# Layer 1 in five token blocks, and remainders stacked along the contraction

## The chip, the cores and the metric

The kernel runs on one core of a Trainium2 chip. The metric is the device time of one execution in microseconds (us), as the median of several. TensorE (PE) multiplies matrices, with its weight loads counted apart (PEld); VectorE (DVE), ScalarE (ACT) and GpSimd (POOL) do the elementwise work; SyncE (SP) issues the DMAs.

## The reference

```python
# attention with 8 heads, 4 batches, 576 tokens, head dimension 64
proj = q_or_k @ w_phi;  proj -= max|proj|;  phi = [exp(proj), exp(-proj)]
x = (phi(q) @ (phi(k).T @ v)) / (phi(q) @ sum(phi(k)) + 1e-6)     # heads side by side: 512 wide
# layer 1
u  = x + real(fft(fft(x, axis=tokens), axis=features))
un = (u - mean(u)) / sqrt(var(u) + 1e-6)
x  = u + maximum(un @ w_ch1, 0) @ w_ch2                           # 512 -> 2048 -> 512
# layer 2
u  = x + (maximum(x.T @ w_tok1, 0) @ w_tok2).T                    # over tokens, 576 -> 256 -> 576
out = u + maximum(u @ w_ch1, 0) @ w_ch2                           # 512 -> 1536 -> 512
```

All is float32. The kernel gets this accuracy from a rounded type (`fp32r`): a number is split into a high and a low half (`h`, `l`), and a product is three matmuls, high by high, high by low and low by high.

## The kernel before

Tokens or features lie along the partitions, a batch is 576 tokens, and a half batch of 288 tokens is the unit of a normalization. The stages run one into the other.

The attention fills the first 190 us. Behind each batch follows its Fourier part. `f_fold` adds and subtracts mirrored tokens into `f`, `f_st1` and `f_stx` multiply by a cosine or sine table over the features (plain float32, four matmuls of 129 columns per call of `f_st1`, L624, each of them two records in the trace), and `f_st2` by one over the tokens. The even part has 289 rows and the odd part 287, each in two tiles of 128 rows and a remainder of 33 or 31. `f_stx` makes the remainders (`yxh`, `yxl`). `f_st2` (L672) adds nine matmuls of 290 columns into one bank of PSUM, three for each of the two full tiles and three for the remainder, which fill only about a quarter of the array's rows. It is called five times per batch, 20 times in all, and L677 and L678 add its result to `u`.

`ln` normalizes half a batch. A ones matrix (L920) sums over the 512 features, for the mean and then for the variance. Ahead of it VectorE adds the four feature tiles up (L911, L913; for the later halves ScalarE and GpSimd split the sum for two faster matmuls). VectorE subtracts the mean (L947), ScalarE squares, and after the second matmul come the root (L965 to L974, VectorE and ScalarE) and the product (L978). `ln_out` splits the result into `xh` and `xl` (ScalarE L995, GpSimd L998).

Layer 1 takes eight blocks of 288 tokens in the batch order 1, 2, 3, 0. `ch1` makes one of 16 tiles of 128 hidden features with 12 matmuls (L1015), ScalarE writes `gh` (L1022), VectorE `gl` (L1023), and `ch2` multiplies them by the second weights into four banks, 12 matmuls (L1037 to L1039). A group is four hidden tiles, after which VectorE adds the four banks to `u` (L1042, four additions). So layer 1 has 3072 matmuls of 288 columns and 128 additions. The first three blocks take the groups 0 to 3 in turn, the next three 3 to 0, the last two 0 to 3.

The weights come through "words": SP loads `raw`, ScalarE, VectorE (L1596: one TENSOR_SCALAR and two SCALAR_TENSOR_TENSOR on 128x512) and GpSimd make halves of it. Two groups of four stay in SBUF; the words of groups 2 and 3 are made while the first blocks run, `w_keep` stores them to DRAM (32 DMAs), and `w_fetch` reads a half group of 1 MB back (`w<-wd`, 24 times).

Layer 2 follows: `c_tr` transposes the tokens to the partitions, `c_tok1` multiplies by `w_tok1` with 512 columns (L1340 to L1342), five tiles of tokens for each of four batches, where the fifth has 64 tokens; then `c_tok2`, and from 698 us the channel product of layer 2, which the change leaves as it is.

Nothing of the order is found at run time. A table `ORDER` gives each step of the attention, the Fourier part and the beginning of layer 1 a start number (its scale only sorts), later steps get theirs from `at` and `later`, and all are emitted in the order of these numbers, which is the order in each engine's queue. An engine works its queue strictly in that order, so a wait holds everything behind it.

## Time and profile before

| | us |
|---|---|
| median of 3 runs (990.99, lowest 989.68, highest 991.08) | 990.99 |
| the profiled execution | 991.51 |
| its span, first to last instruction | 989.8 |
| TensorE busy, 98% of the span | 969.8 |
| VectorE busy, 70% | 689.4 |
| ScalarE busy, 43% | 427.5 |
| GpSimd busy, 41% | 407.9 |

Times are of one profiled execution. The busy time of a matmul counts its whole passage, and successive matmuls overlap, so TensorE may be busy with others' tails; what one matmul costs is read from the distance of the starts. "Idle before" is the time in which an engine stood still ahead of an instruction, and the arrow names what released it. The granted TensorE clock is full (1.00 of 2.4 GHz) in every stretch read here.

### The profile page before, as it was taken

Reading aid. Unit: us, or ns where it says so; the run is one execution under the profiler, and the core shown is the slowest. Engines: PE = TensorE matmul, PEld = TensorE weight load, DVE = VectorE, ACT = ScalarE, POOL = GpSimd, SP = SyncE. Lnnn points to the kernel's source line nnn. Section 1 sums busy time; section 2 is a strip of 40 time slices with the busy share of each in tenths; the row PEclk is TensorE's granted clock in tenths of the full one; section 3 lists DMA queues with packets and bytes.
Section 4 is the critical chain, followed back from the end, with each engine's and each line's share of the span. In section 5 each row is a group of like instructions: output and inputs, shape, how many; then the busy total and the mean of one; then the engine's idle time right before and its main releaser. Section 6 shows DMA issues by size and latency. Waiting matters only on the chain.

```text
span 989.8 us, 21218 instructions
## 1 busy us (share of the span) xinstructions
PE 969.8 (98%) x8322; PEld 905.5 (91%) x8322; DVE 689.4 (70%) x1275; ACT 427.5 (43%) x952; POOL 407.9 (41%) x429
## 2 busy tenths in 40 slices
PE   8999999999999999999999999999999999999998
PEld 8677867789988999999999999988899999999997
DVE  6898898998698845545666843467566768766665
ACT  5676566552244322322333322243444456544442
POOL 0150312131144523333445643332366568865651
PEclk9999999999999999999999999999999999999999
DMA  8566666627155723577334597780045455744452
GB/s 315 185 192 227 193 213 198 226 82 256 57 200 172 243 97 109 175 282 271 129 111 151 192 387 282 235 281 1 4 154 181 154 166 165 243 151 150 150 160 96
DMA packets 97727, 179.04 MB, mean 181 GB/s; under 512 B 9316, under 2 KB 53796, under 8 KB 94044
## 3 DMA queue, kind: packets, MB, share of 16 engines
q1 hardware_dynamic: 97468, 177.62, 53.3%
q8 instruction: 66, 1.08, 0.5%
q14 instruction: 33, 0.27, 0.1%
q10 hardware_dynamic: 160, 0.07, 0.0%
HBM read 126.65 MB, written 48.57 MB: 177 GB/s over the span
## 4 chain that ended last, share of the span: by engine, by line
PE 86%; DVE 9%; ACT 2%; issue 2%; POOL 1%; DMA 0%; SPq 0%; DVEq 0%; ACTq 0%; POOLq 0%
PE pw L1015 18%; PE pw L1107 12%; PE pz L1116 11%; PE pw L434 4%; PE pa L550 3%; PE pk L458 3%; PE pk L1038 3%; PE pk L1039 3%; PE pk L1037 3%; PE pa L1037 3%; PE pa L1039 3%; PE pa L1038 3%; DVE t L1596 3%; PE pw L672 3%; PE pa L530 2%; PE pw L497 2%
## 5 line engine op out<-in xcount | busy, mean ns | idle before, releaser
L1015 PE MATMUL pw<-xh,w 128*128 128x288 f32 x896 | 196.7, 295 | 0.0
L1171 DVE TENSOR_TENSOR u<-u,pz 128x576 f32<-128x576 f32 x157 | 118.1, 753 | 61.2 <-PE pz L1116 59.1
L1107 PE MATMUL pw<-x,ring 128*128 128x288 f32 x1008 | 155.4, 297 | 3.2 <-DVE f L1129 3.2
L1023 DVE SCALAR_TENSOR_TENSOR gl<-pw,gh 128x288 fp32r<-128x288 f32 x128 | 58.1, 455 | 133.3 <-ACT gh L1022 132.9
L1022 ACT ACTIVATE gh<-pw 128x288 fp32r<-128x288 f32 x128 | 52.2, 411 | 227.5 <-PE pw L1015 203.9
L1015 PEld LDWEIGHTS pw<-xh,w 128*128 128x128 f32 x896 | 149.9, 188 | 0.2
L1116 PE MATMUL pz<-g,ring 128*128 128x288 f32 x966 | 149.3, 298 | 0.6 <-DVE u L1171 0.5
L1107 PEld LDWEIGHTS pw<-x,ring 128*128 128x128 f32 x1008 | 139.5, 188 | 6.5 <-DVE f L1129 4.6
L1116 PEld LDWEIGHTS pz<-g,ring 128*128 128x128 f32 x966 | 134.3, 188 | 4.3 <-DVE u L1171 3.3
L1015 PE MATMUL pw<-xl,w 128*128 128x288 f32 x448 | 132.2, 295 | 0.0
L1596 DVE SCALAR_TENSOR_TENSOR t<-raw,t 128x512 uint32<-128x512 uint32 (+3 forms) x130 | 100.9, 781 | 2.2
L1596 POOL TENSOR_TENSOR g<-t,g 128x288 fp32r<-128x288 f32 (+1 forms) x69 | 71.0, 1030 | 42.1 <-ACT g L1142 42.1
L1015 PEld LDWEIGHTS pw<-xl,w 128*128 128x128 f32 x448 | 84.1, 188 | 0.1
L1596 ACT ACTIVATE f<-f 128x288 f32<-128x288 f32 x72 | 32.0, 444 | 116.3 <-DVE f L1129 115.9
L1596 POOL TENSOR_TENSOR g<-f,g 128x288 fp32r<-128x288 f32 x69 | 57.0, 841 | 59.5 <-ACT g L1142 59.4
L1038 PE MATMUL pk<-gl,w 128*128 128x288 f32 x256 | 76.3, 298 | 3.3 <-DVE gl L1023 3.1
L1037 PE MATMUL pk<-gh,w 128*128 128x288 f32 x256 | 76.4, 299 | 1.7 <-DVE u L1042 0.9
L1039 PE MATMUL pk<-gh,w 128*128 128x288 f32 x256 | 75.7, 296 | 0.0
L1037 PE MATMUL pa<-gh,w 128*128 128x288 f32 x256 | 75.6, 295 | 0.0
L1039 PE MATMUL pa<-gh,w 128*128 128x288 f32 x256 | 75.4, 295 | 0.0
L1038 PE MATMUL pa<-gl,w 128*128 128x288 f32 x256 | 75.1, 293 | 0.0
L768 POOL TENSOR_TENSOR wst<-t,wst 128x512 fp32r<-128x512 f32 x16 | 21.4, 1344 | 117.7 <-ACT wst L765 117.7
(212 smaller groups left out, 2095.5 us busy)
## 6 DMA issues: line engine op xcount, KB each, us to landing
w<-wd SPq DMA_DIRECT2D x24, 1024.0 KB, 5.7
ring<-wd SPq DMA_DIRECT2D x24, 1024.0 KB, 5.5
raw<-in_w SPq DMA_DIRECT2D x32, 512.0 KB, 5.5
ring<-wd SPq DMA_DIRECT2D x24, 512.0 KB
wd<-wst SPq DMA_DIRECT2D x22, 448.0 KB, 4.4
wd<-raw SPq DMA_DIRECT2D x22, 448.0 KB, 3.0
wd<-wst SPq DMA_DIRECT2D x18, 512.0 KB, 3.9
wd<-w SPq DMA_DIRECT2D x32, 256.0 KB, 2.8
```

Source lines behind the costliest of these rows:

```text
L434: nc.tensor.matmul(ps[j][:, (t - t0) * 128:(t - t0 + 1) * 128], x[h], T["w"][h], start=True, stop=True)
L458: nc.tensor.matmul(out[g:g + 64], e[:, g:g + 64], v, start=first, stop=last)
L1015: nc.tensor.matmul(out, w[:, k, fs], x[:, k, :], start=(n == 0), stop=(n == 11))
L1022: nc.scalar.activation(out=gh, in_=out, func=AF.Relu)
L1023: nc.vector.scalar_tensor_tensor(out=gl, in0=out, scalar=0.0, in1=gh, op0=ALU.max, op1=ALU.subtract)
L1037: nc.tensor.matmul(out, wh[:, f % 4, ds], gh, start=(f == f0), stop=False)
L1038: nc.tensor.matmul(out, wh[:, f % 4, ds], gl, start=False, stop=False)
L1039: nc.tensor.matmul(out, wl[:, f % 4, ds], gh, start=False, stop=last)
L1107: nc.tensor.matmul(out, w[:, kk, hw], x[XI[i]][:, hx, kk], start=(start and k == 0), stop=(stop and k == 5), skip_group_check=(i != 2))
L1116: nc.tensor.matmul(o[s], w[:, s, hw], g[hx], start=(start and k == 0), stop=(stop and k == 2), skip_group_check=(i != 2))
L1171: nc.vector.tensor_tensor(out=u, in0=u, in1=o, op=ALU.add)
L1596: fn(*a, **k)
```

## The change

The blocks of layer 1 become five, of 512, 512, 512, 480 and 288 tokens, across the borders of batches (`BLOCKS`). Blocks 0 and 1 are done first (`ROUND1`): block 0 with group 0, in two parts of 288 and 224 columns; block 1 with groups 0 and 1; block 0 with 1 and 2; block 1 with 2 and 3; block 0 with 3. Blocks 2, 3 and 4 follow with groups 3 and 2, and again with 1 and 0. Except for the first and last of round 1, eight hidden tiles are accumulated before `u` is added to. An addition is cut where a block crosses two batches. `w_keep` goes; groups 2 and 3 stay, and 0 and 1 are fetched again, group 1 half way through block 4.

Block 1 needs the fourth half, (2, 1), so its normalization joins the three early ones, with its product on GpSimd. Batch 0 is read back as `u0`, normalized from that copy between its spill and its use, stored (`un`) and loaded again before its blocks.

In the Fourier part `f_three` copies the remainder's columns of `f` three times side by side (two ScalarE copies per batch). `f_stx` thus leaves three copies of the 33 or 31 rows, of which `hi` and `third` make (high, high, low), and the table's remainder holds (high, low, high). One matmul over 99 or 93 rows then does what three did: seven in place of nine in `f_st2`. In the token product the fifth tile of 64 tokens is stacked in the same way in two copies, four matmuls in place of six per batch, with one more ScalarE copy (`c_two`).

```diff
-ps_open/a/k -99.600, opn/cv -99.500, a_open -99.000, a_warm/12#2 -98.100, a_load/0/k/0 -98.090, a_load/0/k/1 -98.080,
+ps_open/a/k -99.600, a_open -99.500, thirds -99.000, opn/cv -98.100, a_load/0/k/0 -98.090, a_warm/12#2 -98.080,
...
+    def third(out, src, k, w, n):
+        nc.vector.scalar_tensor_tensor(out=out, in0=src, scalar=T["z"][0:n, k, w:w + 1], in1=out, op0=ALU.mult, op1=ALU.add)
...
+    def f_three(b):
+        need(("fold", b, 0), ("fold", b, 1))
+        for w in range(2):
+            s0, n = (COS_T, SIN_T)[w][2]
+            a, e = (3, 5) if w else (0, 3)
+            nc.scalar.copy(out=T["fx"][:, a:e, 0:3 * n].rearrange("p a (r t) -> p a r t", r=3),
+                           in_=T["f", b][:, a:e, s0:s0 + n].unsqueeze(2).to_broadcast([128, e - a, 3, n]))
+        mark("three", b)
...
+                    nc.tensor.matmul(ps[0:3 * n, par * 129:(par + 1) * 129], T["fx"][:, fi, 0:3 * n],
...
+        def hi():
+            for w, n, ps, y in out:
+                nc.scalar.activation(out=y, in_=ps, func=AF.Copy, scale=T["z"][0:n, 2, w:w + 1])
+            mark("hi", "y", b)
+
+        def lo():
+            need(("hi", "y", b))
+            for w, n, ps, y in out:
+                third(y, ps, 0, w, n)
+            mark("y", b)
+        later(V('da', 1.0), hi)
+        later(V('db', 1.5), lo)
...
-            yh, yl = (y[:, w if st_ == 2 else st_] for y in T[("yx", b) if st_ == 2 else ("y", b, w)])
-            for y, c in ((yh, ch), (yh, cl), (yl, ch)):
-                nc.tensor.matmul(ps[0:m, 0:290], y[:, k0:k0 + m], c[:, st_, :],
-                                 start=(n == 0), stop=(n == 8))
+            if st_ == 2:
+                prods = [(T["yx"][:, w], ch)]
+            else:
+                yh, yl = (y[:, st_] for y in T["y", b, w])
+                prods = [(yh, ch), (yh, cl), (yl, ch)]
+            for y, c in prods:
+                nc.tensor.matmul(ps[0:m, 0:290], y[:, k0:k0 + m], c[:, st_, :], start=(n == 0), stop=(n == 6))
...
-    def w_keep(g, which, k):
-
-        if (0, g, which) not in WD:
-            WD[0, g, which] = dr.tile([2, 128, 4, 512], F32, name=f"wd0{g}{which}")
-        need(("w", 0, g, which, k))
-        mark("wd", ("w", 0, g, which, k))
-        for c in range(2):
-            nc.sync.dma_start(out=WD[0, g, which][c][:, k], in_=W[0, g][which][c][:, k].bitcast(F32))
...
-    FIRST = [(1, 0), (1, 1), (2, 0)]
+    FIRST = [(1, 0), (1, 1), (2, 0), (2, 1)]
+    BLOCKS = [[(1, 0, 512)], [(1, 512, 64), (2, 0, 448)], [(2, 448, 128), (3, 0, 384)], [(3, 384, 192), (0, 0, 288)],
+              [(0, 288, 288)]]
+    ROUND1 = [(0, (0,)), (1, (0, 1)), (0, (1, 2)), (1, (2, 3)), (0, (3,))]
...
+        u = (U[b] if b else T["u0"])[:, :, hf * HB:(hf + 1) * HB]
...
-            (nc.vector if (b, hf) in FIRST else nc.gpsimd).tensor_tensor(out=c, in0=c, in1=r.unsqueeze(1).to_broadcast([128, 4, HB]), op=ALU.mult)
+            (nc.vector if (b, hf) in FIRST[:3] else nc.gpsimd).tensor_tensor(out=c, in0=c, in1=r.unsqueeze(1).to_broadcast([128, 4, HB]), op=ALU.mult)
+            if b == 0:
+                spill["un", hf] = dr.tile([128, 4, HB], F32, name=f"un{hf}")
+                return later(V('us', 2.0), nc.sync.dma_start, out=spill["un", hf], in_=c)
...
+    def parts(blk, g):
+        return [(0, 288), (288, 224)] if blk == 0 and g == 0 else [(0, NB[blk])]
...
+    def u0_load():
+        P["ln"] = pool("ln", 1, "right")
+        T["u0"] = P["ln"].tile([128, 4, S], F32, name="u0")
+        nc.sync.dma_start(out=T["u0"], in_=spill[0])
+
+    def un_load(hf):
+        T["un", 0, hf] = P["tmp"].tile([128, 4, HB], F32, tag="c", name="un")
+        nc.sync.dma_start(out=T["un", 0, hf], in_=spill["un", hf])
...
+                o = -c0
+                for b, t, n in BLOCKS[blk]:
+                    lo, hi = max(o, 0), min(o + n, w_)
+                    if lo < hi:
+                        u = U[b][:, d, t + lo - o:t + hi - o]
+                        nc.vector.tensor_tensor(out=u, in0=u, in1=out[:, lo:hi], op=ALU.add)
+                    o += n
...
+    def c_two(b):
+        t = T["ud", b] = P["cb"].tile([128, 4, 2, 64], F32, tag="ud", name="ud")
+        nc.scalar.copy(out=t, in_=U[b][:, :, 512:576].unsqueeze(2).to_broadcast([128, 4, 2, 64]))
...
-            nc.tensor.matmul(out, h1[0:n, kt, cs], h[0:n], start=(kt == 0), stop=False)
-            nc.tensor.matmul(out, h1[0:n, kt, cs], l[0:n], start=False, stop=False)
-            nc.tensor.matmul(out, l1[0:n, kt, cs], h[0:n], start=False, stop=(kt == 4))
+            nc.tensor.matmul(out, h1[:, kt, cs], h, start=(kt == 0), stop=False)
+            if kt < 4:
+                nc.tensor.matmul(out, h1[:, kt, cs], l, start=False, stop=False)
+            nc.tensor.matmul(out, l1[:, kt, cs], h, start=False, stop=(kt == 4))
...
-    NS = 3
-    for n in range(NS):
-        at(zl + V(f'ln{n}', (36, 54, 74)[n]), ln, *blocks[n], (0, 1, 1)[n])
-        at(zl + V(f'lo{n}', (50, 68, 90)[n]), ln_out, *blocks[n], "dve" if n == 0 else "pool")
...
+    for n, (h, gs) in enumerate(ROUND1):
+        ts = t0
+        t0 = chan(0, t0, four(*gs), h, V(f'fb{n}', (8.0, 5.4, 5.18, 5.18, 5.18)[n]))
...
-    tx = {}
-    for g in (3, 2, 1, 0):
-        for h in ((3, 4, 5) if g else (5, 3, 4)):
-            tx.setdefault(h, t0)
-            chan(0, t0, list(range(4 * g, 4 * g + 4)), blocks[h], fin=(g == 0))
-            t0 += 4 * FT
-        if g > 1:
-            refill(g - 2, t0)
...
+    for h, gs in ((2, (3, 2)), (3, (2, 3)), (4, (3, 2)), (2, (1, 0)), (3, (0, 1)), (4, (1, 0))):
+        ts = t0
+        t0 = chan(0, t0, four(*gs), h)
+        if h == 4 and gs[0] > 1:
+            refill(1, (ts + t0) / 2)
+            refill(0, t0)
+        if h == 2:
+            tb3 = t0
...
+    at(zend + V('p00', 50.0), ln, 0, 0, 2)
+    at(zend + V('p01', 84.0), ln, 0, 1, 2)
+    tcv2 = zend + V('p02', 118.0)
+    at(tcv2, rel, "ln")
+    at(tcv2 + 0.1, opr, "cv2")
+    at(tb2 - 78, ln, 3, 0, 2)
+    at(tb2 - 42, ln_out, 3, 0, 0)
+    at(tb2 - 39, ln, 3, 1, 2)
+    at(tb2 - 6, ln_out, 3, 1, 0)
+    at(tb2 - 5.5, ln_out, 3, 1, 1)
+    at(tb2 + 2, un_load, 0)
+    at(tb2 + 14, ln_out, 0, 0, 0)
+    at(tb2 + 17, un_load, 1)
+    at(tb2 + 30, ln_out, 0, 1, 0)
```

The first place is TensorE at one `f_st2` in the attention. `sch` and `scl` are the halves of the cosine table, `yh`, `yl`, `yxh`, `yxl` those of the first product. Before:

```order
L624 MATMUL pw<-dsin,f 128x129 x4
L672 MATMUL pw<-sch,yh 128x290
L672 MATMUL pw<-scl,yh 128x290
L672 MATMUL pw<-sch,yl 128x290
L672 MATMUL pw<-sch,yh 128x290
L672 MATMUL pw<-scl,yh 128x290
L672 MATMUL pw<-sch,yl 128x290
L672 MATMUL pw<-sch,yxh 128x290
L672 MATMUL pw<-scl,yxh 128x290
L672 MATMUL pw<-sch,yxl 128x290
```
and now:
```order
L569 MATMUL pa<-qe,kz_104 64x288 x4
L716 MATMUL pw<-sch,yh 128x290
L716 MATMUL pw<-scl,yh 128x290
L716 MATMUL pw<-sch,yl 128x290
L716 MATMUL pw<-sch,yh 128x290
L716 MATMUL pw<-scl,yh 128x290
L716 MATMUL pw<-sch,yl 128x290
L716 MATMUL pw<-sch,yx 128x290
```
Nine matmuls of 290 columns are seven, the last with the stacked `yx`.

The second place is VectorE just behind the last Fourier sums of batch 2 (L677, now L720). Before:

```order
L677 TENSOR_TENSOR u<-u,pw 128x289
L678 TENSOR_TENSOR u<-u,pw 128x287
L695 COPY u<-x_3650 1x576
L1042 TENSOR_TENSOR u<-u,pk 128x288 x2
L1042 TENSOR_TENSOR u<-u,pa 128x288 x2
L657 TENSOR_TENSOR yl<-pw,yh 128x258
L1023 SCALAR_TENSOR_TENSOR gl<-pw,gh 128x288 x2
L677 TENSOR_TENSOR u<-u,pw 128x289
L678 TENSOR_TENSOR u<-u,pw 128x287
L677 TENSOR_TENSOR u<-u,pw 128x289
L678 TENSOR_TENSOR u<-u,pw 128x287
L677 TENSOR_TENSOR u<-u,pw 128x289
```
and now:
```order
L720 TENSOR_TENSOR u<-u,pw 128x289
L721 TENSOR_TENSOR u<-u,pw 128x287
L738 COPY u<-x_3547 1x576
L996 TENSOR_TENSOR c<-u,pw 128x1152
L697 TENSOR_TENSOR yl<-pw,yh 128x258 x2
L960 TENSOR_TENSOR sq<-sq 128x576
L962 TENSOR_TENSOR s_3625<-sq 128x288
L1080 SCALAR_TENSOR_TENSOR gl<-pw,gh 128x224
L1014 TENSOR_SCALAR v<-pw 128x288
L1021 TENSOR_TENSOR yy<-rr,v 128x288
L1022 SCALAR_TENSOR_TENSOR yy<-yy,rr 128x288
L1023 SCALAR_TENSOR_TENSOR rr<-yy,rr 128x288
```
Where additions of block sums (L1042) and `gl` stood, the fourth normalization now stands, up to its root. `s_3625` is what the fourth variance matmul on TensorE reads.

The third place is VectorE in layer 1 while the words of groups 2 and 3 are made. `t` is a word, `gl` the low half that `ch2` reads. Before:

```order
L1596 SCALAR_TENSOR_TENSOR t<-raw,t 128x512 x2
L1042 TENSOR_TENSOR u<-u,pk 128x288 x2
L1042 TENSOR_TENSOR u<-u,pa 128x288 x2
L1023 SCALAR_TENSOR_TENSOR gl<-pw,gh 128x288
L1596 TENSOR_SCALAR t<-t 128x512
L1596 SCALAR_TENSOR_TENSOR t<-raw,t 128x512 x2
L1023 SCALAR_TENSOR_TENSOR gl<-pw,gh 128x288
L1596 TENSOR_SCALAR t<-t 128x512
L1596 SCALAR_TENSOR_TENSOR t<-raw,t 128x512 x2
L1023 SCALAR_TENSOR_TENSOR gl<-pw,gh 128x288
L1596 TENSOR_SCALAR t<-t 128x512
```
and now:
```order
L1672 SCALAR_TENSOR_TENSOR t<-raw,t 128x512 x2
L1080 SCALAR_TENSOR_TENSOR gl<-pw,gh 128x512
L1672 TENSOR_SCALAR t<-t 128x512
L1672 SCALAR_TENSOR_TENSOR t<-raw,t 128x512 x2
L1080 SCALAR_TENSOR_TENSOR gl<-pw,gh 128x512
L1672 TENSOR_SCALAR t<-t 128x512
L1672 SCALAR_TENSOR_TENSOR t<-raw,t 128x512 x2
L1080 SCALAR_TENSOR_TENSOR gl<-pw,gh 128x512
```
Between two `gl` there stands one set of words as before, but each `gl` now serves 24 matmuls of 512 columns, not of 288, and four additions no longer follow every fourth.

## Rows read from the trace of the kernel before

**Rows 1.** the page: busy time of each engine, and the chain's shares by engine
```profile
PE 969.8 (98%) x8322; PEld 905.5 (91%) x8322; DVE 689.4 (70%) x1275; ACT 427.5 (43%) x952; POOL 407.9 (41%) x429
...
PE 86%; DVE 9%; ACT 2%; issue 2%; POOL 1%; DMA 0%; SPq 0%; DVEq 0%; ACTq 0%; POOLq 0%
```

**Rows 2.** windows: stretch from:to, its length, then busy us of each engine, PEclk, DMA
```profile
20.00:190.00 170.00, 166.61 (x2336) 127.09 (x2332) 151.81 (x326) 111.65 (x269) 41.40 (x38) 1.00 0.66 213
192.00:234.00 42.00, 42.00 (x328) 36.24 (x325) 39.76 (x77) 20.70 (x40) 11.73 (x7) 1.00 0.45 139
234.00:264.00 30.00, 30.00 (x231) 29.45 (x231) 19.79 (x49) 6.08 (x14) 2.67 (x1) 1.00 0.28 105
260.00:340.00 80.00, 74.97 (x548) 72.92 (x547) 73.84 (x113) 31.96 (x63) 36.80 (x23) 1.00 0.61 194
340.00:360.00 20.00, 20.00 (x153) 20.00 (x152) 9.18 (x19) 5.62 (x12) 7.72 (x11) 1.00 0.36 129
641.00:698.00 57.00, 56.20 (x342) 49.13 (x342) 38.42 (x67) 22.52 (x40) 15.04 (x13) 1.00 0.39 133
```

**Rows 3.** PE's waits in 200 to 345 us: us in total, times, longest
```profile
PE pk L1038 <- DVE gl L1023: 3.1, 4, 1.0
```

**Rows 4.** PE timeline, second product of a 288-column block: start us, us, instruction
```profile
441.25 0.29 PE L1037 MATMUL pk<-gh,w 128*128 128x288 f32 x1
...
447.62 0.29 PE L1037 MATMUL pk<-gh,w 128*128 128x288 f32 x1
```

**Rows 5.** PE timeline, six matmuls of `c_tok1`, 512 columns
```profile
689.22 0.40 PE L1340 MATMUL pk<-yth,t1h 128*128 128x512 f32 x1
...
690.38 0.39 PE L1342 MATMUL pk<-yth,t1l 128*128 128x512 f32 x1
```

**Rows 6.** the chain of waits, a run of `f_st2` and one `f_st1`: start us, us, what
```profile
238.87 3.62 PE pw L672 x27
242.49 0.89 PE pw L624 x8
```

**Rows 7.** VectorE's waits in 20 to 190 us
```profile
DVE m L439 <- PE pw L434: 7.4, 15, 1.4
```

**Rows 8.** VectorE's groups by form: busy us, mean ns, idle before
```profile
L1596 DVE SCALAR_TENSOR_TENSOR t<-raw,t 128x512 uint32<-128x512 uint32 x112 | 91.7, 823 | 1.8
L1023 DVE SCALAR_TENSOR_TENSOR gl<-pw,gh 128x288 fp32r<-128x288 f32 x128 | 58.1, 455 | 133.3 <-ACT gh L1022 132.9
...
L1596 DVE TENSOR_SCALAR t<-t 128x512 uint32<-128x512 uint32 x56 | 33.4, 600 | 4.0 <-ACT t L727 3.3
...
L1042 DVE TENSOR_TENSOR u<-u,pk 128x288 f32<-128x288 f32 x64 | 26.2, 447 | 6.0 <-PE pk L1039 5.8
...
L1348 DVE SCALAR_TENSOR_TENSOR hl<-pk,hh 128x512 fp32r<-128x512 f32 x8 | 5.5, 691 | 4.5 <-ACT hh L1347 4.5
```

**Rows 9.** VectorE timeline, two of the early variance sums
```profile
191.98 0.46 DVE L913 TENSOR_TENSOR s<-sq 128x288 f32<-128x288 f32 x1
...
233.63 0.46 DVE L913 TENSOR_TENSOR s<-sq 128x288 f32<-128x288 f32 x1
```

**Rows 10.** PE timeline, the matmul of those two variance sums
```profile
192.86 0.65 PE L920 MATMUL pw<-s,ones 128*128 128x288 f32 x2
...
234.82 0.65 PE L920 MATMUL pw<-s,ones 128*128 128x288 f32 x2
```

**Rows 11.** GpSimd's groups by form: low half, and product of a normalization
```profile
L998 POOL TENSOR_TENSOR xl<-c,xh 128x1152 fp32r<-128x1152 f32 x6 | 16.8, 2797 | 7.6 <-ACT xh L995 4.0 <-PE pa L1039 3.7
...
L978 POOL TENSOR_TENSOR c<-c,rr 128x1152 f32<-128x1152 f32 x5 | 13.5, 2703 | 10.6 <-DVE rr L974 10.6
```

**Rows 12.** ScalarE's groups by form: cast of a normalized half, and a PSUM copy
```profile
L995 ACT CAST xh<-c 128x1152 fp32r<-128x1152 f32 x7 | 8.0, 1149 | 0.0
...
L485 ACT COPY kz<-pk 128x260 f32<-128x260 f32 x16 | 5.8, 385 | 4.2 <-PE pk L458 4.2
```

**Rows 13.** the page: fetch of one layer-1 weight half, KB and us each
```profile
w<-wd SPq DMA_DIRECT2D x24, 1024.0 KB, 5.7
```

More of the change, by code (lines that the diff above doesn't have):

```diff
@@ L403, in a_split_consts, with rest @@
         for i, (s0, n) in enumerate(tl):
-            nc.sync.dma_start(out=raw[0:n, i, :], in_=src[s0:s0 + n, :])
-            later(5 + 2 * i, split, h[:, i, :], l[:, i, :], raw[:, i, :], "dve", "pool")
+            for a in range(3 if i == 2 else 1):
+                nc.sync.dma_start(out=raw[a * n:a * n + n, i, :], in_=src[s0:s0 + n, :])
+            if i < 2:
+                later(5 + 2 * i, split, h[:, i, :], l[:, i, :], raw[:, i, :], "dve", "pool")
+        def rest():
+            nc.scalar.activation(out=h[:, 2], in_=raw[:, 2], func=AF.Copy, scale=T["z"][:, 3, w:w + 1])
+            third(h[:, 2], raw[:, 2], 1, w, 128)
+        later(9, rest)
     def a_warm(n):
@@ L701, in u_store @@
         if b == 1:
-            need(*[("y1", b, h) for h in range(2)])
+            need(*[("y1", blk, g, c0) for blk, gs in ROUND1 for g in gs[-1:] for c0, _ in parts(blk, g)])
         spill[b] = dr.tile([128, 4, S], F32, name=f"sp{b}_{len(spill)}")
@@ L998, in lo, with ch1 @@
             (nc.gpsimd if le == "pool" else nc.vector).tensor_tensor(out=l, in0=src, in1=h, op=ALU.subtract)
[L999 removed]
+            mark("x", blk, b, hf)
         later(1.4, lo)
[L1003 to L1007 removed]
+    def ch1(m, blk, f, c0, w_):
+        need(*[("x", blk, b, hf) for b in range(B) for hf in range(2) for i, o, _, n in pieces(b, hf)
+               if i == blk and o < c0 + w_ and c0 < o + n],
+             *[("w", m, f // 4, 0, k) for k in range(4)])
+        h, l = T["x", blk]
         wh, wl = W[m, f // 4][0]
         ps = pw()
[L1010 removed]
+        out = ps[:, 0:w_]
         fs = slice((f % 4) * 128, (f % 4) * 128 + 128)
@@ L1014, in ch1 @@
             for w, x in ((wh, h), (wh, l), (wl, h)):
-                nc.tensor.matmul(out, w[:, k, fs], x[:, k, :], start=(n == 0), stop=(n == 11))
+                nc.tensor.matmul(out, w[:, k, fs], x[:, k, c0:c0 + w_], start=(n == 0), stop=(n == 11))
                 n += 1
-        gh = P["b"].tile([128, HB], F32R, tag="gh", name="gh", bufs=3)
-        gl = P["b"].tile([128, HB], F32R, tag="gl", name="gl", bufs=3)
-        T["g", m, b, hf, f] = (gh, gl)
+        gh, gl = (P["b"].tile([128, 512], F32R, tag="g" + c, name="g" + c, bufs=3)[:, 0:w_] for c in "hl")
+        T["g", m, blk, f, c0] = (gh, gl)
         def relu():
@@ L1304, in c_open @@
         for c in range(2):
-            nc.gpsimd.memset(t1[c][0:64, 4].bitcast(F32), 0.0)
+            if c:
+                nc.gpsimd.memset(t1[c][64:128, 4].bitcast(F32), 0.0)
             for i, (t0, n) in enumerate(WT):
-                nc.sync.dma_start(out=t1[c][128 - n:128, i].bitcast(F32), in_=WD["t1", i][0:n, c, 0:256])
+                for h in range(0, n if c else 128, n):
+                    nc.sync.dma_start(out=t1[c][h:h + n, i].bitcast(F32), in_=WD["t1", i][0:n, c, 0:256])
             for i in range(2):
@@ L1422, in mixer_kernel @@
             if w == 0:
+                at(o + 0.5, f_three, b)
                 at(o + gap * 2, f_stx, b)
@@ L1549, in mixer_kernel @@
         t0 = tc_ + 1 + CT * n
+        at(t0 + V('cu', -2.0), c_two, b)
         for kt in range(5):
```

607 lines of the change are left out of this document (301 added, 306 removed), and 5 rows, old and new, of the table PRM.

## The prediction

> **What bounds the kernel now.** I read the page first, for the shares [rows 1]: TensorE is busy 98% of the span and is 86% of the chain that ended last, VectorE 9%. So matmuls that go are worth their price, except where another engine is already as full. Windows by stage show where that is [rows 2]. From 192 to 234 us VectorE has 39.76 us of work in 42, from 260 to 340 us 73.84 in 80, in the attention 151.81 in 170. From 340 us it has air, and TensorE runs without a gap. In 260 to 340 us TensorE starts 548 matmuls, against 4 x 153 = 612 at the pace of 340 to 360 us: 64 too few, or 8.5 us at 0.1327 each, of which its own idle time shows 5.0 (80 - 74.97, an understatement, since a matmul's tail counts as busy). The waits there name VectorE's `gl` [rows 3]. I read this stretch as 5 to 8 us of waiting.
>
> The price of a matmul comes from starts. Of 288 columns, 48 take 447.62 - 441.25 = 6.37 us, 0.1327 each [rows 4]. Of 512 columns, five steps take 690.38 - 689.22 = 1.16 us, 0.232 each [rows 5]. The line through both is 0.000443 us per column, which puts 224 columns at 0.104 and 480 at 0.218, if nothing else changes with the width.
>
> **The change part by part.** The profiled execution took 991.51 us, 1.7 more than its span and 0.5 above the median; the sum is made on it, and the half microsecond is less than I can resolve.
>
> Layer 1, TensorE. Before: 3072 x 0.1327 = 407.7 us. After: block 0's group 0 is 96 matmuls of 288 and 96 of 224, blocks 0 to 2 otherwise 1056 of 512, block 3 384 of 480, block 4 384 of 288: 1056 x 0.232 + 96 x 0.104 + 384 x 0.218 + 480 x 0.1327 = 245.0 + 10.0 + 83.6 + 63.7 = 402.3. That is -5.4. The two starts [rows 5] are rounded to 0.01, so 0.232 is good to 0.002 and the term to 3 us either way.
>
> The Trainium skill has a rule on this ("TensorE: Matmul & The Clock Gate", section "Wait — 56ns, not 53.3ns?"): a warm matmul starts N/2.4 GHz plus about 2.5 ns after the one before, 122.5 ns at 288 and 215.7 at 512. By it the same sum is -2.6, half of mine. The starts here lie 10 and 16 ns above that [rows 4, 5], so the measured steps decide; the rule warns that the overhead saved per wider matmul may be smaller than two rows suggest.
>
> Fourier part. 20 calls of `f_st2` lose two matmuls of 290 columns each. Twenty-seven take 3.62 us [rows 6], 0.134 each, so 40 x 0.134 = -5.4. This holds where TensorE decides. In the attention VectorE is 89% busy and waits only 7.4 us for TensorE's projections [rows 7], so part of the gain there may be met by VectorE; I keep 5.4 here and let it weigh in the new wait below.
>
> Here the Trainium skill speaks against the change: "Perfetto Trace Analysis", section "Identifying the Most-Contended Engine", calls matmul busy time a poor measure of TensorE's load and prefers that of the weight loads. In the attention the weight loads are busy 127.09 of 170, 75%, below VectorE's 89% [rows 2]. By that reading VectorE is the fuller engine there and this term would be worth nothing before 190 us.
>
> Token product: 4 batches x 2 matmuls of 512, 8 x 0.232 = -1.9; TensorE is busy 56.20 of 57 us there, VectorE 38.42 [rows 2].
>
> The waits of 260 to 340 us. After the change one hidden tile of 512 tokens occupies TensorE for 24 x 0.232 = 5.57 us. VectorE has in it one set of words, 2 x 0.823 + 0.600 = 2.25 us, one `gl` of 512, for which the nearest row is 0.691, and at most a piece of a normalization of some 2.4: 5.3 in all [rows 8]. Per 288 tokens it had 2.25 + 0.455 and, every fourth time, 4 x 0.447, against 24 x 0.1327 = 3.18. So the waits should go; of 7 to 8 us I take -7. The bounds are 0 and -8.5.
>
> The early normalizations, the new cost. In 192 to 234 us the sums of VectorE reach TensorE just in time: they end at 192.44 and 234.09, and the matmuls that read them start at 192.86 and 234.82 [rows 9, 10]. The change takes work from TensorE ahead of the third of these variance matmuls: 72 matmuls of layer 1 (the third block no longer begins there) and 30 of `f_st2`, 72 x 0.1327 + 30 x 0.134 = 13.6 us. VectorE loses only four additions and three `gl`, 4 x 0.447 + 3 x 0.455 = 3.2 [rows 8]. TensorE thus comes some 10 us early and waits; up to 3.4 of that can vanish if VectorE itself runs earlier because TensorE did (half of the 7.4 above). From there to block 1's first matmul TensorE has 96 x 0.104 + 28 x 0.134 + 3 of small things = 17 us. VectorE has some 13 us up to the fourth variance sum, by its rows in the order and the durations of the same forms, and then a chain without cover: the matmul 0.65 [rows 10], five root steps of about 0.45 (the form of L1023, 288 columns), the product on GpSimd 2.70, and for the 160 of 288 tokens that block 1 takes of this half a cast of 1.149 x 160/288 = 0.64 and a low half of 2.797 x 160/288 = 1.55 [rows 11, 12]: 7.8. That is 21 against 17, 4 more. So the new wait is 7 + 3 to 10 + 4, 10 to 14 us; I take +12. Its outer bounds are 0, if VectorE's idle 2.2 us [rows 2] and the earlier attention absorb it, and 24, if VectorE in this chain idles as in 234 to 264 us (10.2 of 30) over the 36 us concerned.
>
> The price of 224 columns. No matmul in the rounded type is narrower than 288 columns in this trace. The narrow ones here are plain float32: four of 129 columns take 0.89 us [rows 6], 0.222 each or 1.72 ns per column, 3.9 times the wide rate. The 96 new ones therefore cost between 0.104 and 224 x 1.72 = 0.386 each, 10.0 or 37.1 us in all. I take the low end, because the nearest row in type and width is that of 288, and keep the high one as a rival.
>
> Edits at nothing. The 32 stores of `w_keep` have no one waiting for them; the DMA engines are 0.61 busy there [rows 2], bound -1 to 0. The spill and reload of batch 0 go the same way. The refill of group 1 is issued half a block ahead: four hidden tiles of 24 matmuls, 12.7 us, against 2 x 5.7 us for two fetches one after the other [rows 13], so 1.3 to spare, and up to +6 if they queue behind the words' loads. The eight copies of `f_three` take about 0.385 each [rows 12], on an engine with 58 of 170 us idle: 0 to +3. `third` stands where the subtraction for the low half stood. The four copies of `c_two` have 34 of 57 us of idle ScalarE as cover: 0 to +4.6.
>
> Sum: 991.5 - 5.4 - 5.4 - 1.9 - 7 + 12 = 983.8, forecast 984 us. Own range 979 to 989, from the wait of 10 to 14 and 3 us in the width term.
>
> **The rivals.** First, TensorE alone decides: the earlier attention carries VectorE along and no new wait appears. 991.5 - 19.7 = 972, with 969 to 978 for a wait of up to 6. For it: TensorE is 86% of the chain. Against: VectorE's 39.76 of 42 us.
>
> Second, a transfer or VectorE keeps layer 1's waits: words still fall between every two `gl`, 5.3 of 5.57 us leaves little, and a late refill adds. Then -7 is lost, 984 + 7 = 991, within 989 to 993. For it: `gl` is the named waker, and a normalization now lies in the same stretch. Against: the margin is positive, where it was negative.
>
> Third, slower: the 224-column matmuls run at float32's rate. Then 96 x (0.386 - 0.104) = +27.1 us, all in the stretch of the new wait, which they fill: 984 + 27.1 - 12 = 999; without the wait 972 + 27.1 = 999 too. It decides once one of them costs over 0.104 + 19.7/96 = 0.31 us. For it: the only narrow rows cost four times the rate. Against: these are of another type, and the rounded type at 288 to 512 columns shows a single rate. Range 995 to 1003.
>
> **How the numbers follow.** Forecast 0.42, all on TensorE 0.18, waits that stay 0.14, narrow matmuls 0.26. Measurement cannot tell changes under 0.2%, 2 us, from none. Faster are the first two, 0.60, and none of the others; no change is the third, 0.14; slower the last, 0.26. The range takes in both outer cases, 970 to 1001.
>
> **What would show it.** In the profile after, L1073 should step by 0.232 at 512 columns and 0.104 at 224; 0.2 or more there is the third rival. VectorE should be TensorE's releaser ahead of L969 and of block 1's first L1073 at some 215 to 260 us, 10 to 14 us in all; none of it is the first rival. Between block 1's start and the end of the words TensorE should show no wait for `gl`; several microseconds of it, or a DMA as releaser of L1073, are the second. `f_st2` should be seven steps of 0.134. I am wrong if the span ends under 977 or over 988 us.

## The result and the profile after

The changed kernel takes 996.88 us, the median of 7 runs (994.09 to 1000.21), against 990.43 us for the kernel before in the same sessions (7 runs, 989.19 to 991.08). The ratio is 1.0068, 95% interval 1.0050 to 1.0087: 6.4 us slower, where 984 us was forecast. The profiled execution took 998.69 us with a span of 997.0, the second longest of its seven.

The page after shows what the change took away, and that it did not help. The first line is each engine's busy time, the second the chain that ended last.

```profile
PE 964.9 (97%) x7218; PEld 840.2 (84%) x7218; DVE 671.1 (67%) x1175; ACT 425.7 (43%) x923; POOL 409.7 (41%) x433
...
PE 76%; DVE 12%; DMA 4%; ACT 3%; issue 2%; POOL 1%; SPq 0%; DVEq 0%; ACTq 0%; POOLq 0%
```

Against [rows 1], the weight loads fell by 65 us and TensorE's share of the chain from 86 to 76%. VectorE rose from 9 to 12%, and DMA stands there with 4% where it had none. By stages, from the starts of TensorE's first and last instructions of each:

| | before | after | |
|---|---|---|---|
| first `ch1` | 205.98 | 205.18 | -0.8 |
| from there to the first `c_tok1` | 435.10 | 443.62 | +8.5 |
| from there to the first matmul of layer 2's channel product | 56.49 | 56.04 | -0.45 |
| from there to TensorE's end | 288.56 | 288.60 | 0 |

All of the loss lies in layer 1. I added up, there, the usual step of each matmul (the median distance of starts for its line and width over the run), and took the rest of the time as excess. The steps come to 426.8 us before and 419.2 after, so the work shrank by 7.6 us; other matmuls that now fall into the stage take back some of what layer 1's own gain. The excess rose from 8.3 to 24.4 us, by 16.1. Together that is the 8.5 us by which the stage took longer.

The work is cheaper than forecast. The rows are starts on TensorE: 24 matmuls of 512 columns, and 35 of 224 columns.

```profile
264.41 0.39 PE L1094 MATMUL pk<-gh,w 128*128 128x512 f32 x1
...
269.85 0.39 PE L1073 MATMUL pw<-xh,w 128*128 128x512 f32 x1
```
```profile
249.27 0.28 PE L1094 MATMUL pk<-gh,w 128*128 128x224 f32 x1
...
253.18 0.27 PE L1096 MATMUL pa<-gh,w 128*128 128x224 f32 x1
```

512 columns take 5.44/24 = 0.2267 us, not the 0.232 of [rows 5]; 224 take 3.91/35 = 0.112, so the narrow ones run at the wide rate; 480 take 0.2165 (median). With these the matmuls of layer 1 cost 1056 x 0.2267 + 96 x 0.112 + 384 x 0.2165 + 480 x 0.1327 = 397.0 us against 407.7, a gain of 10.7. So the loss is in the waits. First the windows that answer [rows 2]; the token product now lies at 648.8 to 704.8 us.

```profile
20.00:190.00 170.00, 164.80 (x2328) 124.13 (x2327) 154.93 (x325) 115.81 (x281) 38.80 (x35) 1.00 0.65 213
192.00:234.00 42.00, 37.78 (x282) 28.93 (x281) 41.12 (x80) 19.53 (x37) 13.61 (x8) 1.00 0.56 200
234.00:264.00 30.00, 28.39 (x190) 25.15 (x190) 17.89 (x39) 8.01 (x15) 6.97 (x3) 1.00 0.03 10
260.00:340.00 80.00, 76.45 (x331) 62.78 (x330) 44.79 (x70) 22.52 (x39) 18.77 (x14) 0.96 0.23 77
340.00:360.00 20.00, 18.00 (x73) 14.25 (x72) 18.95 (x28) 6.82 (x13) 11.97 (x7) 0.91 0.37 127
648.80:704.80 56.00, 54.97 (x330) 47.24 (x329) 38.80 (x66) 23.22 (x42) 14.92 (x13) 1.00 0.40 136
```

Three things are to be seen. In 192 to 234 us TensorE, without a gap before, is idle for 4.2 us while VectorE has 41.12 us of work in 42. In 260 to 340 us VectorE has only 44.79 of 80, where it had 73.84, and yet TensorE is not full. And the granted clock, 1.00 in every stretch before, is 0.96 and 0.91 there. Nearly all of the excess falls into four places; the rest of the stage is 0.8 us under the medians.

| us after | excess | what it is |
|---|---|---|
| 206 to 242 | 8.1 | TensorE waits for VectorE's sums and foldings |
| 287 to 297 | 6.8 | one wait of 3.5, then 3.3, of which 2.4 at half the clock |
| 344 to 351 | 3.9 | two waits, 2.4, then 1.5 at half the clock |
| 529 to 539 | 6.4 | two waits, 3.4, then 3.0 at the lower clock |

**The second place.** These are TensorE's starts around it.

```profile
286.91 0.39 PE L1073 MATMUL pw<-xh,w 128*128 128x512 f32 x1
290.58 0.61 PE L969 MATMUL pw<-sv,ones_r 128*128 128x288 f32 x1 [3.28 <-ACT sv L1672]
291.46 0.61 PE L969 MATMUL pw<-srr,ones_r 128*128 128x288 f32 x1 [0.27 <-POOL srr L1672]
291.87 0.63 PE L1094 MATMUL pk<-gh,w 128*128 128x512 f32 x1
292.30 0.63 PE L1095 MATMUL pk<-gl,w 128*128 128x512 f32 x1
...
296.56 0.63 PE L1096 MATMUL pa<-gh,w 128*128 128x512 f32 x1
```

L969 is a mean or variance sum, here of batch 0's copy. The wait is put down to ScalarE's half of the sum, but ScalarE waited for VectorE, and VectorE for a transfer. In the chain of waits of the same stretch (start, length, what) and in VectorE's timeline it reads so:

```profile
280.90 0.95 PE pw L716 x7
...
281.90 6.83 DMA u<-sp
...
288.76 0.77 DVE sq L960
```
```profile
288.76 0.76 DVE L960 TENSOR_TENSOR sq<-u 128x576 f32<-128x576 f32 x1 [14.67 <-DMA u<-sp]
```

`u0_load` (L1040) may be issued only when the room of the Fourier part is free, after the last `f_st2` (L716) at 281.9 us. In SyncE's queue it had stood since 225.2 us, as the view of its line shows (durations in ns, then first and last start):

```profile
L1040 SPq EVENT_SEMAPHORE  x1: 56694/56694/56694, 225.2 to 225.2; - x1
L1040 SPq DMA_DIRECT2D u<-sp x1: 320/320/320, 281.9 to 281.9; - x1
```

The copy landed 6.83 us later. Because its first addition stands in VectorE's queue ahead of the last Fourier sums, a `gl` and the words, all of these stood still for 14.7 us, and TensorE with them once its own lead was used up. It is a transfer in front of ready work. The loads of the words stand behind it in SyncE's queue too: the next `raw` went out at 282.26 us, and VectorE began the first word of groups 2 and 3 at 291.99 us, where it was 262.2 in the kernel before. Whether these loads could have gone earlier is not shown; no run moved `u0_load`.

After the wait the 12 matmuls of 512 columns start 0.427 us apart, then 0.227 again. The windows before, in, behind and after it give the granted clock in the third column from the right: 1.00, 0.95, 0.50 (1.2 GHz) and 0.99.

```profile
284.40:287.20 2.80, 2.80 (x13) 2.06 (x11) 0.00 (x0) 0.00 (x0) 0.00 (x0) 1.00 0.95 387
287.20:290.60 3.40, 0.12 (x2) 0.02 (x1) 1.81 (x4) 0.50 (x2) 0.00 (x0) 0.95 0.18 74
290.60:297.00 6.40, 6.13 (x15) 4.60 (x16) 6.26 (x12) 2.77 (x4) 2.09 (x2) 0.50 0.26 81
297.00:300.00 3.00, 3.00 (x14) 2.48 (x13) 1.74 (x3) 0.45 (x2) 0.56 (x1) 0.99 0.44 127
```

**The third place** is the variance sum of batch 3's first half. These are lines of VectorE, GpSimd and TensorE around it.

```profile
342.55 1.84 DVE L960 TENSOR_TENSOR sq<-sq 128x576 f32<-128x576 f32 x1
342.04 1.75 POOL L797 TENSOR_TENSOR w<-t,w 128x512 fp32r<-128x512 f32 x1 [4.51 <-ACT w L794]
345.56 1.36 POOL L1672 TENSOR_TENSOR srr<-s,sv 128x288 fp32r<-128x288 f32 x1 [1.77 <-ACT sv L1672]
345.53 0.40 PE L969 MATMUL pw<-sv,ones_r 128*128 128x288 f32 x1 [0.97 <-ACT sv L1672]
346.97 0.40 PE L969 MATMUL pw<-srr,ones_r 128*128 128x288 f32 x1 [1.03 <-POOL srr L1672]
```

The addition ahead of the first wait lasts 1.84 us beside a product by which GpSimd forms a word's half (L797), where 14 of the 16 on this line take 0.68 to 0.76. GpSimd's part of the sum, ahead of the second, lasts 1.36 us beside VectorE's words, where it took 0.81 at 331.1 us. So each wait follows an instruction that two engines drew out; that this makes the waits is read from the trace, and no run tests it.

**The fourth place** is the refill. TensorE's starts, and SyncE's queue ahead of them:

```profile
529.18 0.29 PE L1096 MATMUL pa<-gh,w 128*128 128x288 f32 x1
530.42 0.50 PE L1073 MATMUL pw<-xh,w 128*128 128x512 f32 x1 [0.95 <-DMA w<-wd]
530.76 0.40 PE L1073 MATMUL pw<-xl,w 128*128 128x512 f32 x1
533.31 1.22 PE L1073 MATMUL pw<-xh,w 128*128 128x512 f32 x2 [2.15 <-DMA w<-wd]
```
```profile
522.24 0.33 SPq L760 DMA_DIRECT2D raw<-in_wt  x1
522.62 0.43 SPq L916 DMA_DIRECT2D wd<-raw  x1
523.15 1.35 SPq L838 DMA_DIRECT2D w<-wd  x2
524.55 2.30 SPq L876 DMA_DIRECT2D raw<-in_w  x3
```

The fetch went out at 523.15 us, six microseconds before its use, behind loads of layer 2's words that waited for their own room, and it shared the DMA engines with them: their busy share was 1.02 in 530 to 540 us, where it had been 0.70 before.

### The profile page after: what moved, and what is told of

Same layout as the page of the kernel before. It is cut to its first block, busy times and chain, and to the rows that moved or that the text cites. A ratio compares the mean times of both kernels' runs of the same rounds, so it can differ in the third digit from the quotient of the medians.

```text
span 997.0 us, 18765 instructions
## 1 busy us (share of the span) xinstructions
PE 964.9 (97%) x7218; PEld 840.2 (84%) x7218; DVE 671.1 (67%) x1175; ACT 425.7 (43%) x923; POOL 409.7 (41%) x433
## 4 chain that ended last, share of the span: by engine, by line
PE 76%; DVE 12%; DMA 4%; ACT 3%; issue 2%; POOL 1%; SPq 0%; DVEq 0%; ACTq 0%; POOLq 0%
PE pw L1073 17%; PE pw L1166 12%; PE pz L1175 11%; PE pa L1094 3%; PE pk L1096 3%; PE pk L477 3%; PE pa L1096 3%; PE pa L1095 3%; PE pw L453 3%; PE pk L1095 3%; PE pk L1094 3%; PE pa L569 2%; PE pw L516 1%; PE pw L716 1%; PE pa L549 1%
## 5 line engine op out<-in xcount | busy, mean ns | idle before, releaser
L1073 PE MATMUL pw<-xh,w 128*128 128x512 f32 (+3 forms) x672 | 198.1, 363 | 4.1 <-DMA w<-wd 3.1
L1080 DVE SCALAR_TENSOR_TENSOR gl<-pw,gh 128x512 fp32r<-128x512 f32 (+3 forms) x84 | 51.2, 613 | 146.2 <-ACT gh L1079 146.1
L1073 PEld LDWEIGHTS pw<-xh,w 128*128 128x128 f32 x672 | 122.7, 190 | 23.7 <-DMA w<-wd 3.8
L1079 ACT ACTIVATE gh<-pw 128x512 fp32r<-128x512 f32 (+3 forms) x84 | 44.8, 537 | 217.6 <-PE pw L1073 213.2
L1073 PE MATMUL pw<-xl,w 128*128 128x512 f32 (+3 forms) x336 | 121.4, 361 | 0.0
L458 DVE TENSOR_REDUCE m<-pw 128x4 f32<-128x512 f32 (+1 forms) x96 | 52.6, 547 | 14.2 <-PE pw L453 14.1
L1095 PE MATMUL pk<-gl,w 128*128 128x512 f32 (+3 forms) x168 | 61.3, 365 | 0.2 <-DVE gl L1080 0.2
L1094 PE MATMUL pa<-gh,w 128*128 128x512 f32 (+3 forms) x168 | 61.5, 366 | 0.0
L1094 PE MATMUL pk<-gh,w 128*128 128x512 f32 (+3 forms) x168 | 61.5, 366 | 0.0
L1096 PE MATMUL pk<-gh,w 128*128 128x512 f32 (+3 forms) x168 | 61.3, 365 | 0.0
L1095 PE MATMUL pa<-gl,w 128*128 128x512 f32 (+3 forms) x168 | 61.2, 364 | 0.0
L1096 PE MATMUL pa<-gh,w 128*128 128x512 f32 (+3 forms) x168 | 61.2, 364 | 0.0
```

The source lines that it names most:

```text
L458: nc.vector.tensor_reduce(out=m[:, 0:n], in_=pv[j], axis=AX.X, op=ALU.max, apply_absolute_value=True)
L1073: nc.tensor.matmul(out, w[:, k, fs], x[:, k, c0:c0 + w_], start=(n == 0), stop=(n == 11))
L1079: nc.scalar.activation(out=gh, in_=out, func=AF.Relu)
L1080: nc.vector.scalar_tensor_tensor(out=gl, in0=out, scalar=0.0, in1=gh, op0=ALU.max, op1=ALU.subtract)
L1094: nc.tensor.matmul(out, wh[:, f % 4, ds], gh, start=(f == f0), stop=False)
L1095: nc.tensor.matmul(out, wh[:, f % 4, ds], gl, start=False, stop=False)
```

## The experiments

Theory A was that these are separate waits, each made by one instruction that stands too early or too late in a queue that works in order. Rival B was that VectorE (or the DMA engines) is simply full, so that a wait removed here returns elsewhere. Times are compared with the changed kernel's 996.9 us; every ratio is against runs of the kernel before on the same chip. These came out at 990.1 to 991.3 us from session to session, so a difference between two sessions' times is uncertain by about 1 us.

**Batch 0's normalization later.**
```diff
-u0_load 324.300, ..., ln/0/0/2 329.520,
+u0_load 324.300, ..., ln/0/0/2 340.520,
 ...   (all later steps of ln/0/0 likewise +11)
```


> The changed kernel with one edit: the first half's normalization of batch 0's copy starts 11 later in the order, so that two more hidden tiles and a set of words stand ahead of it on every engine. In the trace of the changed kernel VectorE stood still for 14.7 us at its first addition, until the copy had landed at 288.7 us; TensorE then waited 3.5 us for its sum at 287 us and ran 3.3 us longer at the lower clock. Theory A, the order puts a late transfer ahead of ready work: these 6.8 us go, about 997 - 7 = 990 us, the granted clock stays at 1.00 in 280 to 300 us. Rival B, VectorE is full in 190 to 390 us and only its place of waiting moves: the same 6 to 7 us turn up at gl or at a later variance sum, 995 to 998 us.

Measured: 991.72 us, ratio 1.0003 (0.9993 to 1.0013), 5.2 us less. TensorE no longer waits at all in 280 to 300 us, and the clock holds:

```profile
280.00:300.00 20.00, 20.00 (x93) 16.73 (x93) 11.92 (x18) 5.39 (x10) 3.90 (x3) 1.00 0.39 138
```

A holds. Of the 10.7 us of the second and third place 4.1 remain, as waits of 1.6 and 2.5 us at 321 and 340 us without loss of clock. The load itself, and the loads of words behind it, go out as late as before (282.6 and 283.0 us).

**The refill earlier.**
```diff
-            refill(1, (ts + t0) / 2)
+            refill(1, (ts + t0) / 2 - 2.6)
```


> The changed kernel with one edit: both fetches of group 1's weights are issued 2.6 earlier in the order, ahead of three loads and two stores for layer 2's weights in SyncE's queue. In the trace of the changed kernel TensorE waits for these fetches at 529 to 533 us (3.4 us) and then runs at the lower clock until 539 us (2.2 us). Theory A, the fetch stands behind other transfers in a queue that works in order: 3 to 5.6 us go, 991.5 to 994 us. Rival B, the transfers themselves are limited (the DMA engines are fully busy from 530 to 560 us), so an earlier issue lands little earlier: under 1.5 us, 995.5 to 997 us.

Measured: 992.68 us, ratio 1.0015 (1.0004 to 1.0026), 4.2 us less. The first fetch is now issued at 519.53 us, and what is left of the waits in 500 to 560 us is this:

```profile
PE pk L1096 <- DMA w<-wd: 0.5, 1, 0.5
PE pw L1073 <- DMA w<-wd: 0.5, 1, 0.5
```

A holds: 3.6 us in the queue were enough, although the DMA engines stayed full (share 1.00 in 530 to 540 us).

**Both.** 

> The changed kernel with both earlier edits: batch 0's first normalization 11 later, and group 1's fetches 2.6 earlier in the order. Alone they took 5.2 and 4.2 us off (996.9 to 991.7 and 992.7). Theory A, two separate waits: the gains add, 996.9 - 9.4 = 987.5 us, faster than the kernel before by 3 to 4 us. Rival B, one wait shadows the other (words or VectorE catch up in between): 990 to 991.5 us.

Measured: 987.55 us, ratio 0.9965 (0.9954 to 0.9977). The gains add, 9.3 us where 9.4 were expected; by the ratios, which take out the sessions, it is 1.0% where the two alone give 1.2. So the two waits are independent as far as these runs can tell, and with them mended this version beats both kernels.

**The Fourier product at nine matmuls again.**
```diff
+                if st_ == 1 and n == 6:
+                    for _ in range(2):
+                        nc.tensor.matmul(ps[0:m, 0:290], T["zz"][:, 0:m], ch[:, 0, :], start=False, stop=False)
 ...   (T["zz"] is a tile of zeros; the last of the nine now ends the sum)
```


> The changed kernel with two further matmuls of 290 columns by zeros in each of the 20 calls of the second Fourier product: TensorE's cost of nine is restored, all else stays. Theory A, VectorE set the pace up to some 205 us and the cut bought only what lies behind it: 13 of the 20 calls cost nothing, seven cost 14 x 0.134 = 1.9 us, less where TensorE waits for VectorE anyway: 997 to 999 us. Rival B, TensorE set the pace throughout: 40 x 0.134 = 5.4 us, 1002 us.

Measured: 996.56 us, ratio 1.0052 (1.0041 to 1.0063): over the whole kernel 40 matmuls more cost nothing that can be measured. But the reason of theory A does not hold: they are paid for where they stand. From the 400th projection matmul (`pw<-w,raw`) to the last `pk<-v,ek`, a stretch of the attention, TensorE takes 62.63 us, where the six profiles with the changed kernel's code there take 60.23 to 60.28; the 14 matmuls added in it cost 2.4 us, although VectorE is 91% busy (154.93 of 170). The first `ch1` comes 2.4 us later (207.53; 203.6 to 205.9 in those six). This is won back behind: TensorE's idle time in 192 to 234 us shrinks from 4.2 to 3.1 us, the excess at the wait for batch 0's copy from 6.8 to 4.1, and layer 1 ends at the same time.

**The kernel before with seven.**
```diff
-            for y, c in ((yh, ch), (yh, cl), (yl, ch)):
+            for y, c in ((yh, ch), (yh, cl), (yl, ch))[:1 if st_ == 2 else 3]:
```


> The kernel before, with seven matmuls in the second Fourier product instead of nine: the two products of the remainder that hold a low half are left out. Theory A, VectorE sets the pace up to 206 us: only the 7 calls behind that count, 14 x 0.134 = 1.9 us, 988 to 989.5 us. Rival B, TensorE sets the pace: 5.4 us, 985 us.

Measured: 987.73 us, ratio 0.9961 (0.9948 to 0.9974), 3.5 us less, between the two. By the starts 2.1 us of it come before the first `ch1` and 1.5 behind, a rough split, as one code's profiles differ by 2.4 us there. So the same 40 matmuls were worth two thirds of their price in the kernel before and nothing in the changed one, where TensorE waits away behind them what they gain. A part of that is the wait for batch 0's copy, which the first edit removes; what they are worth with it removed, no run shows.

**A filler in the wait.**
```diff
+            if (b, hf) == (0, 0):
+                ps = pw()
+                for n in range(16):
+                    nc.tensor.matmul(ps, W[0, 0][0][0][:, 0, 0:128], W[0, 0][0][0][:, 1, :], start=(n == 0), stop=(n == 15))
             mu = ln_mean(s1)
```


> The changed kernel with 16 matmuls of 512 columns, whose result nobody reads, ahead of the sum for which TensorE waited 3.5 us at 287 us; they take 16 x 0.227 = 3.6 us and so fill that wait. In the trace of the changed kernel the granted clock fell to half behind the wait, and 12 matmuls of 512 columns took 0.427 us each, not 0.227, which with two more steps is 3.3 us. Theory A, standing still is what costs the clock: it stays at 1.00 there, the wait costs as before, 3 us are gained: 993.5 to 994.5 us. Rival B, the clock falls for another reason (the narrow work before, or the run): nothing gained, 996.5 to 997.5 us; if the filler delays the sum it is 3 us slower than that.

Measured: 994.92 us, ratio 1.0045 (1.0032 to 1.0057), 2.0 us less than the changed kernel, between the two; the intervals overlap, so the finding rests on the trace. In its windows the filler fills 286.7 to 290.5 us, and behind it the clock stays up:

```profile
283.80:286.70 2.90, 2.90 (x14) 2.43 (x13) 0.00 (x0) 0.00 (x0) 0.00 (x0) 1.00 0.99 385
286.70:290.50 3.80, 3.80 (x17) 2.81 (x15) 1.71 (x4) 0.41 (x2) 0.00 (x0) 1.00 0.20 80
290.50:292.00 1.50, 0.41 (x4) 0.42 (x3) 1.50 (x5) 1.08 (x3) 0.80 (x1) 1.00 0.00 0
292.00:298.00 6.00, 6.00 (x28) 4.89 (x28) 5.86 (x10) 1.79 (x2) 1.30 (x1) 1.00 0.25 87
```

So at this place standing still is what cost the clock, and useless work kept it. From the unit ahead of the wait to the next `ch1` it is 284.01 to 294.75, 10.74 us, where the changed kernel took 284.42 to 296.99, 12.57. Of the 1.8 us, 2.4 come from the 12 matmuls behind it, and 0.5 are lost because the sum is read later.

**Batch 0's second half later too.**
```diff
-..., ln/0/1/2 363.520, ...      "p02": 118.0      "c2": 40.06      "c4": 8.86
+..., ln/0/1/2 383.520, ...      "p02": 138.0      "c2": 20.06      "c4": 8.027
```


> As the run with both edits, and the second half of batch 0 is normalized 20 later in the order, so that it no longer interleaves with the first half of batch 3 while words are made; the first words of layer 2 start 20 later. In the run with the first edit alone TensorE waits 1.6 us at 321 us and 2.5 us at 340 us for variance and mean sums there, with VectorE busy throughout. Theory A, three normalizations are crowded into 50 us on a full VectorE: 2 to 4 us less than the run with both edits, 984 to 985.5 us. Rival B, the words alone fill VectorE, the waits move behind 345 us: within 1 us of it.

Measured: 997.93 us, ratio 1.0064 (1.0044 to 1.0085), 10 us more than the run with both edits. A miss, and a badly built one: since the copy's room is where layer 2's words are made, these had to start later and closer together. New waits show in 440 to 560 us, after the place that was to be mended:

```profile
PE pk L1094 <- DVE u L1103: 3.2, 2, 2.9
PE pk L1096 <- DMA w<-wd: 2.6, 1, 2.6
PE pk L1094 <- ACT gh L1079: 1.1, 1, 1.1
```

The run does show one thing about the 4.1 us at 321 and 340 us. The wait at 321 us is gone, but at 339 us TensorE still waits 1.2 and 0.8 us for batch 3's variance sum, without batch 0's second half beside it. So crowding does not make that wait; there, too, the addition ahead of it (L960) lasts 1.85 us beside a word's half on GpSimd.

**VectorE lightened, first way.**
```diff
-                nc.vector.tensor_copy(out=f[:, 2, 0:289], in_=f[:, 0, 0:289])
+                nc.scalar.copy(out=f[:, 2, 0:289], in_=f[:, 0, 0:289])
 ...   (and three smaller copies)
```


> The run with both edits (987.5 us), with four small copies of the Fourier part moved from VectorE to ScalarE: three in each folding, 0.17 to 0.30 us each, and one of 0.45 us in each batch's sums. Between 195 and 243 us that takes 0.8 + 0.9 = 1.7 us from VectorE, whose instructions there follow one another without a gap and make the chain of waits. Theory A, VectorE sets the pace there and TensorE's 8 us of early waits are its backlog: 1.5 us less in that stretch, and up to as much again in the attention, 985 to 986 us. Rival B, the waits are set by the steps between the engines (matmul, square, root), not by VectorE's load, or ScalarE's queue delays the copies: 987.5 us or more.

Measured: 998.53 us, ratio 1.0087 (1.0071 to 1.0104), 11 us more. The long copy reads what VectorE has just written, and VectorE's next instruction writes over one of its rows, so it became a hand-over there and back. VectorE's longest waits in 20 to 260 us:

```profile
DVE m L458 <- PE pw L453: 10.0, 16, 2.2
DVE f L627 <- ACT f L626: 5.6, 4, 2.7
DVE c L996 <- POOL xl L1056: 4.5, 1, 4.5
```

The second and third are not there in the run with both edits, and the first is 7.9 there. The first `ch1` comes at 209.49 us (203.55), and the clock is at 1.2 GHz for 10 us between 235 and 260 us, where it was full. B's second condition, that ScalarE delays the copies, is what these waits show.

**The same, with a third shift of the refill.** 

> As the run before it, with group 1's fetches another 0.6 earlier, ahead of one more store in SyncE's queue. In the run with both edits TensorE still waited 1.35 us for the second of these fetches at 521.5 us. Theory A, each place in the queue counts: 0.5 to 1.3 us less than that run, 984 to 985.5 us. Rival B, the two transfers of 1 MB take the time they take once the slot is free: the same within 0.4 us.

Measured: 1000.1 us, ratio 1.0094 (1.0077 to 1.0112). The copies hide whatever 0.6 did; nothing follows on the refill.

**VectorE lightened, second way.**
```diff
-            acc(t, U[b][0:1, 2, :], 1, ALU.add, ALU.add)
...
-            nc.vector.tensor_copy(out=U[b][0:1, 2, :], in_=T.pop("x256"))
...
-                nc.vector.tensor_tensor(out=f[0:1, 2, 1:288], in0=lo[0:1, 1], in1=rv[0:1, 1], op=ALU.add)
-                nc.vector.tensor_copy(out=f[0:1, 2, 0:289:288], in_=e2[0:1, 1, 0:289:288])
```


> The run with both edits (987.5 us), with one-row work of VectorE left out: the sums for feature 256 (two additions and a copy per batch) and two of the folding's row instructions. The result lacks that feature's share; TensorE's work is unchanged and nothing goes to another engine. VectorE loses 4 x (0.36 + 0.36 + 0.37 + 0.45 + 0.09) = 6.5 us in all by the steps between starts, 2 x 1.1 + 0.45 = 2.6 of them between 195 and 243 us. Theory A, VectorE sets the pace from the attention to block 1: 2.6 us less at least, up to 6.5, 981 to 985 us, and TensorE's waits of 205 to 240 us shrink from 8 to about 5. Rival B, the handing over between engines sets it: 987 to 988 us.

Measured: 984.79 us, ratio 0.9939 (0.9925 to 0.9952), 2.8 us less than the run with both edits: A at its low end. Its profile cannot place it. The excess of 206 to 242 us falls from 8.1 to 6.7 us, and block 1 begins 0.8 us earlier (250.78 for 251.62), but the other five profiles with the changed kernel's code up to there have 7.6 to 9.1 us and begin block 1 at 252.9 to 254.5. In the attention TensorE gains nothing from it: the stretch named above takes 60.23 us. So VectorE's load costs time somewhere; that it sets the waits of 206 to 242 us fits, but is not shown.

## Why the prediction was wrong

**The step that failed** is the paragraph "Edits at nothing", in two of its sentences. "The spill and reload of batch 0 go the same way" (the stores for which no one waits): the reload cost 6.8 us at its place, and moving its first user 11 back in the order gave 5.2 back. I priced the bytes and not the queues. The row that [rows 2] gave for DMA, 0.61 busy, says nothing on when a load may be issued, and neither the room that it needed (free after the last `f_st2`) nor the three queues that stood behind it were followed. The second: the refill with "1.3 to spare". I counted 12.7 us from the half of block 4, but a load and a store of layer 2's weights stood ahead of the fetch in SyncE's queue, and the load waited for its own room until 522.24 us. The fetch was issued six us before its use, and TensorE could go on 7.3 and 10.2 us after the issue, not the 5.7 of [rows 13] or twice that from an earlier start. "up to +6 if they queue behind the words' loads" was there as a bound, and 6.4 is what it cost; I gave the case 0.14.

**The clock was missing from the sum.** About 7 us (2.4 + 1.5 + 3.0) are matmuls at 1.2 GHz behind waits that add up to 2.4 to 3.5 us. The trace of before has no such stretch in layer 1; its longest wait for `gl` is 1.0 us [rows 3]. An added wait has to be priced with what follows it.

**The early normalizations: right mechanism, wrong size.** 8.1 us of waits for VectorE in 206 to 242 us, where 12 were forecast (10 to 14). The part up to the third variance sum was 6.0 (forecast 7 to 10), the part behind it 2.1 (3 to 4).

**The waits for `gl`** went as forecast: 0.2 us is left of the 3.1 in [rows 3]. But they did not leave the stretch free; waits for sums of batch 0 and batch 3 took their place. The second rival came nearest: it had a transfer or VectorE keep the waits, and a late refill, but through `gl`, and to 993 us at most.

**Fourier part, -5.4: wrong.** By the run with nine matmuls again it is worth nothing in this kernel. In the kernel before it was worth 3.5. What failed is not the price in the attention, where 14 matmuls put back cost 2.4 us, but that a gain there reaches the end: TensorE only comes earlier to the waits behind. The Trainium skill ("Perfetto Trace Analysis", section "Identifying the Most-Contended Engine") judges TensorE's headroom by MFU and its weight loads, 75% busy here, below VectorE's 89%. By that reading there would be no gain before 190 us; the trace does not bear it out for that stretch, though the sum over the kernel came out as it said.

**Layer 1's width: too small.** -10.7 from the measured steps, not -5.4; the two starts of [rows 5] gave 0.232, as the token product still shows after the change (0.231 to 0.236), but layer 1 runs at 0.2267. The estimate by the rule of the Trainium skill ("TensorE: Matmul & The Clock Gate", section "Wait — 56ns, not 53.3ns?") was further off, with -2.6. **Token product:** the matmuls' steps fell by 1.8 us (54.9 to 53.1), as forecast, but the excess rose from 1.6 to 2.9, in waits at 671 to 677 us for which I had allowed nothing: -0.45.

**The rivals.** The slower one, narrow matmuls at float32's rate, is refuted (0.112 us). The time came out at its end of the range for another reason: 996.9 lies in the range of 970 to 1001, the sign and the cause lie outside the forecast. My sum set one loss against four gains; the trace holds four places of loss, 25.2 us, where the kernel before lost 8.3 in all. Two slips in the working carry nothing: half of the 7.4 us is 3.7, not 3.4, and by its own rows VectorE's margin per hidden tile was about zero before (3.18 us against 2.25 + 0.455 + 0.447), not negative.
